# Linear attention feeding an MLP on one core: GpSimd waits for VectorE's two-input instructions, one more half block with seven products, and a new written order

## The chip, the cores and the metric

The kernel runs on one core of a Trainium2 chip. A core has five engines that run side by side, each through its own list of instructions in order: TensorE (PE in the profile) multiplies matrices into PSUM, VectorE (DVE) and ScalarE (ACT) work on PSUM and on SBUF, GpSimd (POOL) works on SBUF, and SyncE (SP) only starts DMAs here. They wait for one another by semaphores. The metric is device time in microseconds; lower is better. The median of three runs of the kernel before is 301.77 us (301.6 to 303.27).

## The reference

Eight batches of eight heads go through linear attention with positive random features, and the result through an MLP with x * relu6(x + 3) / 6. Shapes: q, k and v are 8 x 8 x 576 x 64, omega is 128 x 64, the MLP is 512 -> 2048 -> 512 over 8 x 576 = 4608 tokens.

```python
def phi(x):                                   # x is q or k, scaled by 64 ** -0.25
    h = einsum('bhsd,md->bhsm', x, omega) - sum(x * x) / 2
    return exp(h - max(h over m)) / sqrt(128)
kv = einsum('bhsm,bhsd->bhmd', phi(k), v)
z  = sum(phi(k) over s)
x  = einsum('bhsm,bhmd->bhsd', phi(q), kv) / (einsum('bhsm,bhm->bhs', phi(q), z) + 1e-6)
h  = x.reshape(4608, 512) @ w_in
out = (h * clip(h + 3, 0, 6) / 6) @ w_out
```

## The kernel before, in words

**Blocks.** Batch b gives 512 "main" tokens (block b of the MLP) and 64 left over; the left-over tokens of all batches form block 8. `attention(b)` writes the transposed attention output to `xT` (512 features in 4 tiles of 128, by 512 tokens) and the left-overs to `xS`. While TensorE works on the MLP of block b-1, the attention of batch b runs between.

**Attention.** `K`/`Q` (or the bursts `R`, from batch 3 on) project k and q onto omega, ScalarE takes the exponential (`kp`, `qpT`), VectorE the maximum (`mx`) and its reciprocal (`cc`). `vc` is v times `cc`, written by GpSimd or ScalarE, `kv` multiplies `kp` with it, `num` multiplies `qpT` with the result, and VectorE divides (`rec`, `div`). From batch 2 on, transposes are done by DMA, issued on SP.

**First MLP layer.** The 16 groups of 128 hidden units are `f` and `f + 8` for f = 0 to 7. Plainly (`mm1`, L1083) a group takes 4 matmuls of 128x512 and is followed by an activation on ScalarE into `tsb` (L1089) and a product on VectorE into `gT` (L1091). `mm1_quad` (L1248 for its matmuls) does two values of f and f + 8, on two halves of the tokens, by Strassen's method in Winograd's form: seven products of half size in the place of eight. It needs sums of weights (`input_sums`: W1 to W4, VectorE), sums of inputs (`x_sums`: X1 to X4), three copies (`q1`, `q2`, `q3`), two adds (`q4` L1273, `q5` L1276), and ends with four activations (`qr0` to `qr3`, L1284) and four products (`qg0` to `qg3`, L1286). It holds four PSUM banks of eight, X, Y, Z and W. `FIRST7 = (7, 2)` says from which block on: the half with f = 0 to 3 from block 7, the half with f = 4 to 7 from block 2.

**Second MLP layer.** Block 0 is done plainly (`mm2`, L1327). Later blocks use seven products too (`products`, L1415; the last one of block 8 at L1484): `token_sums` and `last_sum` make S1 to S4 out of `gT` (L1343, on GpSimd or VectorE), `plus` adds partial results (L1431), `store` writes out.

**Order.** Nothing is put in order on the chip. Each piece of work is an `Op` with its reads, its writes and an estimate of its time on each engine it may use. `ORDER` holds, for each engine, the numbers of the Ops in the order in which that engine does them; which list an Op is in also settles its engine. `schedule` walks through these lists with the estimates, gives out PSUM banks, and puts fill matmuls (L597) where it finds TensorE idle in the first 21 us. `emit` writes the instructions with a semaphore wait for each dependence that isn't already implied. An Op marked with `port` is one that the planner lets start only when a shared resource of VectorE and GpSimd is free:

```python
                if e in o.port:
                    shared[0] = o.end - (0.07 if e == "POOL" else 0.0)
```

That moves the planned start only; it leaves no wait in the program. DMAs of k and q for batches from 1 on are issued on GpSimd's queue, since they convert to bf16; loads of batches 3 to 7 wait for a named TensorE step of an earlier block (`gates`).

Of the kernel before, what the change touches and what calls it, by code (L numbers as in the profile page):

```python
# [16 lines left out]
EV0 = (("ACT","DVE"), ("ACT","DVE"), ("POOL", "ACT"), {"k": ("POOL", "ACT", "DVE"), "q": ("POOL", "ACT","DVE")})  # L17
# [4 lines left out]
        14, 121, 115, 117, 131, 138, 159, 147, 119, 141, 150, 144, 156, 135, 127, 153, 123, 125, 176, 129, 133, 174,  # L22
        166, 170, 172, 168, 188, 190, 203, 162, 178, 205, 164, 218, 193, 180, 220, 233, 208, 195, 235, 210, 407, 248,
        395, 223, 401, 198, 396, 238, 402, 397, 240, 408, 403, 398, 245, 225, 409, 404, 410, 213, 413, 416, 243, 228,
        271, 419, 291, 251, 422, 425, 428, 431, 275, 281, 434, 277, 437, 279, 318, 440, 443, 273, 309, 446, 315, 306,
        289, 285, 449, 312, 287, 297, 300, 586, 596, 303, 326, 320, 597, 336, 576, 294, 587, 330, 577, 588, 328, 283,
        578, 598, 332, 324, 589, 322, 599, 357, 579, 566, 359, 567, 362, 344, 580, 590, 568, 346, 334, 383, 569, 570,
        571, 349, 370, 385, 591, 365, 572, 581, 375, 372, 388, 600, 601, 592, 582, 583, 352, 391, 593, 573, 378, 602,
        603, 617, 505, 620, 614, 623, 466, 469, 475, 478, 635, 490, 472, 629, 632, 487, 481, 647, 484, 659, 644, 507,
        501, 653, 638, 497, 493, 668, 503, 499, 665, 662, 495, 650, 779, 511, 509, 531, 519, 780, 521, 536, 533, 524,  # L30
        789, 555, 782, 783, 560, 557, 790, 543, 712, 545, 548, 792, 793, 692, 795, 798, 799, 705, 796, 816, 810, 813,
        719, 819, 825, 828, 840, 831, 834, 845, 842, 844, 802, 863, 847, 803, 868, 849, 851, 865, 744, 870, 867, 732,
        987, 874, 737, 997, 734, 988, 872, 768, 756, 746, 1003, 749, 761, 990, 758, 998, 773, 770, 991, 1000, 1001, 900,
        1004, 1006, 1007, 913, 1018, 1024, 1021, 920, 1010, 1027, 1033, 927, 1039, 1050, 1048, 1036, 1011, 1042, 1053,
        1071, 1052, 1073, 1055, 1076, 1057, 1075, 952, 1059, 1078, 1080, 1195, 940, 976, 1082, 942, 957, 1196, 945, 954,
        1205, 964, 1198, 969, 966, 1199, 1206, 978, 981, 1121, 1208, 1209, 1108, 1214, 1215, 1128, 1229, 1232, 1226,
        1241, 1135, 1235, 1244, 1256, 1247, 1250, 1261, 1258, 1260, 1211, 1263, 1279, 1212, 1265, 1284, 1267, 1283,
        1281, 1218, 1286, 1403, 1404, 1290, 1148, 1160, 1219, 1150, 1165, 1288, 1184, 1162, 1153, 1406, 1413, 1414,
        1329, 1189, 1407, 1186, 1172, 1416, 1174, 1177, 1336, 1417, 1419, 1420, 1316, 1422, 1423, 1440, 1437, 1434,
        1452, 1464, 1449, 1443, 1466, 1468, 1469, 1458, 1455, 1471, 1426, 1473, 1427, 1343, 1475, 1487, 1356, 1611,  # L40
        1491, 1492, 1358, 1380, 1489, 1361, 1494, 1382, 1368, 1612, 1370, 1498, 1496, 1373, 1614, 1392, 1621, 1615,
        1622, 1537, 1394, 1397, 1385, 1624, 1625, 1544, 1627, 1628, 1551, 1630, 1634, 1631, 1524, 1635, 1642, 1645,
        1672, 1648, 1651, 1657, 1660, 1677, 1674, 1676, 1663, 1564, 1576, 1679, 1566, 1578, 1569, 1666, 1681, 1695,
        1581, 1683, 1588, 1699, 1600, 1590, 1697, 1593, 1700, 1722, 1702, 1602, 1723, 1605, 1704, 1706, 1753, 1732,
        1725, 1776, 1726, 1733, 1757, 1758, 1755, 1781, 1735, 1760, 1736, 1762, 1764, 1778, 1780, 1783, 1741, 1799,
        1742, 1787, 1785, 1738, 1804, 1801, 1824, 1803, 1806, 1822, 1739, 1808, 1810, 1826, 1827, 1745, 1876, 1829,
        1746, 1831, 1833, 1878, 1845, 1881, 1880, 1901, 1846, 1883, 1899, 1885, 1848, 1904, 1903, 1849, 1887, 1924,
        1906, 1922, 1908, 1855, 1927, 1926, 1856, 1910, 1929, 1945, 1858, 1931, 1949, 1933, 1950, 1859, 1861, 1947,
        1862, 1952, 1864, 1978, 1865, 1956, 1968, 1969, 1868, 1869, 1954, 1979, 1984, 1971, 1981, 1982, 1985, 1972,
        1988, 1989, 1997, 2003, 2000,  # L50
    ],
    "SP": [
        0, 18, 22, 33, 20, 23, 26, 25, 24, 27, 28, 32, 29, 30, 31, 262, 260, 261, 465, 464, 462, 463, 461, 459, 460,
# [72 lines left out]
        1390, 1462, 1485, 1619, 1463, 1509, 1640, 1638, 1641, 1560, 1575, 1559, 1574, 1562, 1654, 1402, 1587, 1586,  # L126
        1598, 1656, 1655, 1669, 1692, 1670, 1749, 1715, 1874, 1728, 1717, 1671, 1694, 1731, 1730, 1729, 1796, 1872,
        1797, 1873, 1819, 1875, 1774, 1844, 1821, 1843, 1896, 1898, 1851, 1897, 1775, 1919, 1853, 1852, 1921, 1854,
        1944, 1965, 1976,
    ],  # L130
}

# [288 lines left out]
def _emit(nc, es, q, k, v, omega, w_in, w_out, out):  # L421
# [803 lines left out]
    def mm1_quad(blk, f):  # L1225
# [11 lines left out]
        def bank(v):  # L1237
            return v.ring.t[v.slot]
# [373 lines left out]
```

## Time and profile before

| what | value |
|---|---|
| median of 3 runs | 301.77 us (301.6 to 303.27) |
| the profiled execution's own time | 302.46 us |
| its span, first to last instruction | 300.6 us |
| busy: PE / DVE / ACT / POOL | 292.2 / 271.4 / 212.9 / 206.3 us |
| matmuls | 2899 |
| granted TensorE clock | 1.00 |
| moved by DMA | 44.90 MB |

The span lies within the profiled execution's time. In the profile's groups, a name such as `p` or `gT` is a tile with its number left out, `p` being PSUM; `out<-in` says what is written from what. "Idle before" is the idle time of the engine just ahead of the instruction, with what ended it. A line number is that of the kernel before; one helper line can stand for several uses, so L1343 holds all sums of weights, inputs and hidden units, and L543/L544 all copies.

### The profile page before, as it was taken

What the parts mean: (1) busy time and instruction counts of PE and PEld (TensorE: products, weight loads), DVE (VectorE), ACT (ScalarE), POOL (GpSimd) and SP (SyncE); (2) the same over time, 40 slices, a digit from 0 to 9 for tenths busy, and PEclk for the clock granted to TensorE, in tenths of its full rate; (3) what the DMA queues carried; (4) which work ended last, traced back from release to release, by engine and by line L of the source; (5) the groups of instructions that cost most, each with busy time, mean ns of one, the idle gap of its engine ahead of it and who ended that gap; (6) DMA issues with size and microseconds to landing.
All of it is one profiled execution on the core that took longest, in us unless ns stands there. A gap on an engine that the chain in (4) does not pass through costs nothing.

```text
span 300.6 us, 7551 instructions
## 1 busy us (share of the span) xinstructions
PE 292.2 (97%) x2899; PEld 222.1 (74%) x2899; DVE 271.4 (90%) x593; ACT 212.9 (71%) x479; POOL 206.3 (69%) x226
## 2 busy tenths in 40 slices
PE   7999999999999999999989999999999999999996
PEld 5688955554884798569736887588757788888885
DVE  4889898889999998999879998999999999997875
ACT  2975899199878992997587776985887576687310
POOL 1664827039898986589939869998279939869711
PEclk9999999999999999999999999999999999999999
DMA  7999999999999997799769898999531600300034
GB/s 234 292 188 168 266 200 127 197 215 155 242 110 234 126 191 138 173 139 196 171 169 172 144 241 129 106 200 220 86 94 57 166 0 3 126 16 0 2 143 140
DMA packets 90100, 44.90 MB, mean 149 GB/s; under 512 B 57936, under 2 KB 87760, under 8 KB 90064
## 3 DMA queue, kind: packets, MB, share of 16 engines
q1 hardware_dynamic: 62064, 30.71, 46.1%
q0 software_dynamic: 26592, 12.46, 33.7%
q10 hardware_dynamic: 1408, 1.25, 1.3%
q8 instruction: 23, 0.38, 0.5%
q14 instruction: 13, 0.11, 0.1%
HBM read 36.73 MB, written 9.44 MB: 154 GB/s over the span
## 4 chain that ended last, share of the span: by engine, by line
PE 81%; DVE 8%; ACT 5%; POOL 5%; issue 1%; POOLq 0%
PE p L1415 29%; PE p L1248 15%; PE p L1083 11%; PE p L1327 5%; PE p L1302 4%; PE p L1014 3%; PE p L986 2%; DVE mx L820 2%; PE p L796 2%; POOL s L1343 2%; PE p L597 2%; ACT kp L847 2%; PE p L860 2%; POOL vc L970 1%; PE p L840 1%; PE p L799 1%
## 5 line engine op out<-in xcount | busy, mean ns | idle before, releaser
L1284 ACT ACTIVATE tsb<-p 128x512 f16<-128x512 f32 x72 | 41.4, 601 | 21.8 <-PE p L1248 12.0
L1083 PE MATMUL p<-xT,wi 128*128 128x512 f16 x224 | 53.1, 379 | 1.8 <-ACT qpT L824 1.4
L1286 DVE SCALAR_TENSOR_TENSOR gT<-tsb,p 128x512 f16<-128x512 f16 x72 | 46.8, 676 | 3.0 <-ACT tsb L1284 2.8
L1415 PE MATMUL p<-wo,gT 128*128 128x256 f16 x368 | 47.0, 273 | 0.0
L1083 PEld LDWEIGHTS p<-xT,wi 128*128 128x128 f16 x224 | 21.3, 98 | 24.9 <-ACT qpT L824 2.1
L1091 DVE SCALAR_TENSOR_TENSOR gT<-tsb,p 128x512 f16<-128x512 f16 x56 | 36.4, 674 | 3.1 <-ACT tsb L1089 2.8
L1415 PEld LDWEIGHTS p<-wo,gT 128*128 128x128 f16 x368 | 34.8, 98 | 4.9 <-issue 0.5
L1089 ACT ACTIVATE tsb<-p 128x512 f16<-128x512 f32 x56 | 33.2, 620 | 7.0 <-PE p L1083 5.3
L543 ACT COPY p<-p 128x512 f32<-128x512 f32 x55 | 32.2, 599 | 4.1 <-PE p L1415 2.0
L970 POOL TENSOR_TENSOR vc<-v,cc 128x512 bf16<-128x512 f32 x27 | 28.7, 1061 | 7.1 <-DVE cc L964 5.2
L824 ACT ACTIVATE qpT<-p 128x512 bf16<-128x512 f32 (+1 forms) x50 | 27.7, 577 | 6.8 <-PE p L799 6.8
L1343 POOL TENSOR_TENSOR gT<-gT,s 128x512 f16<-128x512 f16 x21 | 24.3, 1157 | 12.0 <-PE p L1415 10.6
L1415 PE MATMUL p<-t,gT 128*128 128x256 f16 x256 | 31.8, 273 | 0.4 <-DVE u L1431 0.4
L1343 POOL TENSOR_TENSOR gT<-gT 128x512 f16<-128x512 f16 x24 | 28.2, 1177 | 4.7 <-DVE s L1343 3.2
L815 ACT ACTIVATE kp<-p 128x512 bf16<-128x512 f32 (+1 forms) x50 | 26.8, 571 | 5.9 <-PE p L799 5.6
L820 DVE TENSOR_REDUCE mx<-kp 128x4 f32<-128x512 bf16 (+1 forms) x50 | 29.3, 618 | 0.3 <-ACT kp L815 0.3
L643 POOL DMA_DIRECT2D kb<-in_k_dram x21 | 16.2, 774 | 18.8 <-PE p L1083 18.1
L1030 DVE TENSOR_TENSOR xb<-p,rec 128x384 f16<-128x384 f32 (+1 forms) x64 | 28.2, 467 | 0.3
L1415 PEld LDWEIGHTS p<-t,gT 128*128 128x128 f16 x256 | 24.3, 98 | 5.4 <-issue 1.3
L1343 POOL TENSOR_TENSOR s<-gT,s 128x512 f16<-128x512 f16 x21 | 24.4, 1164 | 3.4 <-DVE s L1343 2.2
L1343 POOL TENSOR_TENSOR s<-gT 128x512 f16<-128x512 f16 x19 | 22.0, 1158 | 4.7 <-DVE gT L1286 3.1
L643 POOL DMA_DIRECT2D qb<-in_q_dram x28 | 19.6, 713 | 7.5 <-PE p L1083 5.0
(139 smaller groups left out, 671.4 us busy)
## 6 DMA issues: line engine op xcount, KB each, us to landing
v<-in_v_dram SPq DMA_DIRECT2D x14, 512.0 KB, 4.8
out_dram<-osb SPq DMA_DIRECT2D x14, 512.0 KB, 3.3
kb<-in_k_dram POOLq DMA_DIRECT2D x14, 256.0 KB, 5.0
qb<-in_q_dram POOLq DMA_DIRECT2D x14, 256.0 KB, 5.6
wo<-in_moe_w_out_dram POOLq DMA_DIRECT2D x8, 256.0 KB, 9.9
wi<-in_moe_w_in_dram POOLq DMA_DIRECT2D x3, 512.0 KB, 7.5
q<-in_q_dram SPq DMA_DIRECT2D x4, 256.0 KB, 4.8
vl<-in_v_dram SPq DMA_DIRECT2D x8, 128.0 KB, 4.2
```

The source lines that it names most:

```text
L543: return E.copy(dst(), src())
L643: lambda E: E.dma_start(dst, src), prio + 0.001 * turn_of[0], reads=gate, writes=keys,
L820: op("DVE", dvet(128 * (d1 - d0)), lambda E, ko=ko, mo=mo: E.reduce_max(mo, ko, axis=AX.X), p0 + 0.01, reads=[("kp", 0, d, lh) for d in ra ...
L970: return E.tensor_tensor(vcm[:, :, 0:D], v32[:, m, :, :], cbc, ALU.mult)
L1083: ins = E.matmul(ring.t[vh.slot], wi[:, c, 128 * f:128 * f + 128], xv[:, c, :], start=(c == 0), stop=(c == NJ - 1))
L1089: op("ACT", actt(512), lambda E: E.activation(tsb[tu][:], ring.t[vh.slot], AF.Relu, bias=0.5, scale=1.0 / 6.0), t - 0.1, reads=[vh], write ...
L1091: op("DVE", dvet(512), lambda E: E.scalar_tensor_tensor(gT[gu][:, f, :], tsb[tu][:], 1.0, ring.t[vh.slot], ALU.min, ALU.mult), t - 0.1, re ...
L1248: ins = E.matmul(bank(v)[:, 256 * g:256 * g + 256], w(c, f + g), x[:, c, :], start=start and g == 0 and c == 0, stop=c == 1, skip_group_ch ...
L1284: op("ACT", actt(512), lambda E, v=v, tu=tu: E.activation(tsb[tu][:], bank(v), AF.Relu, bias=0.5, scale=1.0 / 6.0), t - 0.1, reads=[v], wr ...
L1286: op("DVE", dvet(512), lambda E, v=v, tu=tu, dst=dst: E.scalar_tensor_tensor(dst, pieces(tsb[tu][:]), 1.0, pieces(bank(v)), ALU.min, ALU.m ...
L1343: op(engines, {"POOL": 0.1 + n / 475.0, "DVE": 0.09 + n / 2000.0}, lambda E: E.tensor_tensor(dst, x, y, ALU.subtract if minus else ALU.add ...
L1415: ins = E.matmul(ring.t[v.slot][:, 256 * j:256 * j + 256], a[:, f, 128 * j:128 * j + 128], w[:, f, :], start=(first and f == 0 and j == 0) ...
```

## The change

1. `schedule` remembers the last VectorE Op that is marked with `port` (`holder`). A GpSimd Op with `port` that the walk puts after it, and within 4 us of its end, gets a dependence on it, which `emit` turns into a semaphore wait where no other wait covers it. GpSimd is also planned to start 0.15 us after such a VectorE Op.
2. `FIRST7` and `QUAD` go from (7, 2) to (7, 1): the half with f = 4 to 7 of block 1 is done by `mm1_quad`. The sums of its weights are made before.
3. `q5` writes its sum to the SBUF tile `p7` and no longer to PSUM bank W; `qr2` and `qg2` read it there, and `qg2` is marked with `port="DVE"`.
4. In batch 0, `vc` is made in two halves, each on GpSimd, VectorE or ScalarE.
5. The loads of batches 3 to 7 lose their `gates`.
6. Several estimates of time change, and `ORDER` is a new one for all five engines.

```diff
-EV0 = (("ACT","DVE"), ("ACT","DVE"), ("POOL", "ACT"), {...})
+EV0 = (("ACT","DVE"), ("ACT","DVE"), ("POOL", "ACT", "DVE"), {...})
 ORDER = {
...
+        holder = None
...
                 if e in o.port:
-                    shared[0] = o.end - (0.07 if e == "POOL" else 0.0)
+                    shared[0] = o.end - (0.08 if e == "POOL" else -0.15)
+                    if e == "DVE":
+                        holder = o
+                    elif holder is not None and st - holder.end < 4.0:
+                        o.deps.setdefault(holder, False)
...
-        op(EV_VC if b else V0, {...}, e_vc, t, port=("POOL", "DVE"), reads=[("cc", pb, m), ("v32", 0, m), ("v32", 1, m)], writes=[("vc", u2, 0)], name="vc" + nm)
+        for hs in ([0], [1]) if b == 0 else ([0, 1],):
+            i0, i1 = 4 * hs[0], 4 * hs[-1] + 4
...
-    FIRST7 = (7, 2)
-    QUAD = (7, 2)
+    FIRST7 = (7, 1)
+    QUAD = (7, 1)
...
-            return v.ring.t[v.slot]
+            return v.ring.t[v.slot] if isinstance(v, Virt) else p7[v[1]][:]
...
-        op("DVE", dvet(512), lambda E: E.tensor_tensor(bank(W), bank(Z), p7[w7][:], ALU.add), t - 0.1, reads=[("p7", w7), Z], writes=[W],
-           name="q5." + nm)
+        op("DVE", dvet(512), lambda E: E.tensor_tensor(p7[w7][:], bank(Z), p7[w7][:], ALU.add), t - 0.1, reads=[Z],
+           writes=[("p7", w7)], name="q5." + nm)
...
-        for n, (v, i, k_) in enumerate(((X, 0, 0), (Y, 1, 0), (W, 1, 1), (Z, 0, 1))):
+        for n, (v, i, k_) in enumerate(((X, 0, 0), (Y, 1, 0), (("p7", w7), 1, 1), (Z, 0, 1))):
...
-               t - 0.1, reads=[v, ("t", tu)], writes=[...], name="qg%d.%s" % (n, nm))
+               t - 0.1, reads=[v, ("t", tu)], writes=[...], name="qg%d.%s" % (n, nm),
+               port="DVE" if n == 2 else ())
...
-            load(b, (), {"k": [("m1", b - 2, 2)], "q": [("m1", b - 2, 4)], "v": [("m1", b - 2, 9)]})
+            load(b, (), {t: [] for t in "kqv"})
...
+            for h in range(2):
+                if FIRST7[h] == 1:
+                    input_sums(h)
```

## The prediction

> **What bounds the kernel now.** I read the page first: busy shares, then the 40 slices, then the idle time by stretch, then the waits of TensorE alone.
>
> ```profile
> span 300.6 us, 7551 instructions
> PE 292.2 (97%) x2899; PEld 222.1 (74%) x2899; DVE 271.4 (90%) x593; ACT 212.9 (71%) x479; POOL 206.3 (69%) x226
> PE   7999999999999999999989999999999999999996
> DVE  4889898889999998999879998999999999997875
> ```
>
> TensorE (PE) is full from the second slice to the last but one, VectorE (DVE) is at 90%, and ScalarE (ACT) and GpSimd (POOL) have room. A busy TensorE need not run at its pace, so I compare instruction starts: a 128x512 matmul follows the one before after 0.216 us, a 128x256 one after 0.109 us. In the chain of work that ended last, eight 128x256 matmuls take 0.87 us, or 0.109 us each. TensorE's stream sets the time, and what can be won is a shorter stream or fewer holes in it. The holes, by stretch of the span (columns: length, then busy us of each engine):
>
> ```profile
> 0.00:22.50 22.50, 20.16 (x204) 15.60 (x205) 15.95 (x51) 14.85 (x35) 11.64 (x21) 1.00 1.07 238
> 60.00:150.00 90.00, 89.83 (x907) 64.77 (x906) 85.23 (x188) 74.13 (x174) 71.85 (x76) 1.00 1.04 174
> 150.00:240.00 90.00, 87.48 (x908) 64.39 (x906) 84.88 (x188) 68.39 (x153) 68.20 (x74) 1.00 0.81 149
> 292.50:300.60 8.10, 5.30 (x57) 4.59 (x54) 4.71 (x9) 0.00 (x0) 1.16 (x1) 1.00 0.40 130
> 60.00:94.00 34.00, 34.00 (x307) 22.29 (x306) 31.71 (x68) 29.97 (x70) 25.86 (x28) 1.00 1.05 191
> ```
>
> Of 8.4 us without a matmul, 2.3 lie in the start, 2.8 in the tail, and about 3.2 inside, most of them in 150 to 240 us. What ended them, in TensorE's waits:
>
> ```profile
> PE p L1083 <- ACT qpT L824: 1.4, 1, 1.4
> PE p L1415 <- POOL s L1343: 0.7, 1, 0.7
> PE p L1083 <- DVE gT L1091: 0.4, 1, 0.4
> PE p L1415 <- DVE u L1431: 0.4, 1, 0.4
> ```
>
> A hole hides some 0.16 us more, since the matmul ahead of it is drawn 0.27 us long at a pace of 0.11. Six holes are then worth 3.2 + 1.0 = 4.2 us. They come from VectorE, GpSimd or ScalarE being late. One cause of lateness can be seen directly:
>
> ```profile
> 237.97 1.16 POOL L1343 TENSOR_TENSOR q<-xT 128x512 f16<-128x512 f16 x1
> 238.19 1.22 DVE L1343 TENSOR_TENSOR s<-gT,s 128x512 f16<-128x512 f16 x1
> ```
>
> VectorE's sum takes 0.41 us where GpSimd is quiet. Here GpSimd started 0.22 us earlier, and the sum ends 0.28 us after GpSimd does. The same happens at 278.94 us (1.41 us), just ahead of the hole that `u` ends. The 55 two-input sums of 512 elements on VectorE (L1343) cost 30.8 us, not 55 x 0.41 = 22.7: 8.1 us are lost in this way, 0.15 us per sum.
>
> **The change part by part.**
>
> *Seven products in the second half of block 1's hidden units.* TensorE loses 32 matmuls of 128x512 and gains 56 of 128x256 by the two programs' instruction lists: 32 x 0.216 = 6.91 against 56 x 0.109 = 6.10, so 0.81 us less on the path. No clearing matmul is added. The weight sums W1 to W4 were there before; W1 of this half (at 88 us, 0.68 us of VectorE) only moves ahead. New on other engines: four adds `q4`, `q5` (4 x 0.69), four input sums (X2, X3 on VectorE, X1, X4 on GpSimd at 1.16 each) and six copies on ScalarE (0.60 each, 3.6 us, while 3 output copies of block 0 leave that stretch). From the first to the second block's first `gT` write VectorE has 72 instructions, not 65. At the pace of 0.60 us of back-to-back instructions the extra is 4 x 0.60 for the adds, 1.7 for two S1 sums, one S4 and one X2, 0.6 for X1 of the next block, 0.6 for one more maximum, less W1 and two `kvz`: about 4.0 us. VectorE idles 34.00 - 31.71 = 2.3 us in 60 to 94 us. So it becomes full there, and a lateness of up to 1.7 us, 2.5 us with the shorter TensorE stretch, has to be made good later. This is the dear part.
>
> *`q5` writes p7 in SBUF instead of the PSUM bank W; `qr2`, `qg2` read it there (20 each).* The bank comes free after `q3`, not after `qg2`, a gain that I can't price alone. ScalarE's 20 activations read SBUF. The near rows are 128x64 from SBUF at 342 ns and 128x130 from PSUM at 276; less 0.79 ns an element (`qpT`: 618 ns for 512, 416 for 256), the fixed parts are 291 and 173 ns, so 0.12 us more each. The Trainium skill ("VectorE: DVE Perf Modes", The TRN2 errata) gives ScalarE 224 cycles of fixed cost from SBUF and 172 from PSUM, 0.04 us more each. By the row that is 2.4 us, by the page 0.9 us, both over 300 us of an engine with 88 us idle; I take the row, since it holds this kernel's form with a scale, and charge the path nothing. On VectorE the page would make `qg2` 62 cycles cheaper from SBUF, 20 x 0.065 = 1.3 us. The rows deny it: 128x256 from PSUM (409 ns) and an unhindered 128x512 two-input sum from SBUF at two elements a cycle (410) have the same fixed part. I take 0.
>
> *Waits.* GpSimd instructions that wait on VectorE go from 54 to 83 of some 147 computing ones. A GpSimd start follows the VectorE end that it waits for by 0.07 us (a sum at 283.87 of 0.41 us, GpSimd at 284.35), so 29 x 0.07 = 2 us of GpSimd, beside its 94 idle ones; its instructions fall by some 10 us besides (12 fewer 512-element sums of gT and s at 1.16). Behind a waiting instruction stand the next sums and the k and q loads on the same queue; those loads now have no TensorE gate (18.1 + 5.0 us of waits before), so they come no later. If that cover is gone, a late S sum holds TensorE as at 238 us. What the waits buy: GpSimd no longer takes the port ahead of a VectorE instruction that stands before it. The Trainium skill ("SBUF — State Buffer", Who interferes with whom) says that a VectorE instruction with two SBUF inputs contends with GpSimd's reads, and that the first to issue holds the pair. The row at 238 us agrees, and the page speaks against one part: `qg2` now has two SBUF inputs, where before one lay in PSUM. At 0.15 us each that is 20 x 0.15 = 3.0 us new blocking against 8.1 us of old, of which waits can remove only what GpSimd took out of turn. Taking a half, 4 us, the two nearly cancel: -1 us of VectorE in sum, from +3 (nothing removed) to -8 (all removed, `qg2` free).
>
> *New sequence.* VectorE's instruction counts by their rows give about +3 us (4 fewer PSUM copies in the products, 10 fewer copies of transposes, 4 new adds, 12 more S sums), ScalarE +10 us, GpSimd -10 us. The start keeps its TensorE work and gets 3 more fill matmuls (3 x 0.11 = 0.3 us of idle that they cover), while two ScalarE copies of 1.05 us (`vcl`) leave the chain at 12.9 us for GpSimd. Bounds of its effect are -1.0 and +1.0 us; I take 0. The tail can be read: before, the last TensorE instruction ended at 297.80 us, its VectorE part at 298.13, the last store was issued by 298.71. Afterwards the second half of product 5 stands only one 0.45 us product ahead of the end, so C21 (0.69 us) ends 0.44 us after TensorE, and its two stores (0.57 us each, both on SP) are out 0.47 + 1.14 = 1.6 us after it instead of 0.9: +0.7 us on the path (bounds 0.2 and 0.9). SP keeps its 114 instructions; loads, transposes and stores swap places by one or two. No wait of TensorE on a transpose of x or of k and q is in the list above, so that is hidden; if one came late, it would cost up to the 1.2 us that such a transpose takes to issue on SP.
>
> *Holes.* The 4.2 us inside are partly port blocking (238, 280 and, behind GpSimd's DMA issues, 160 us: 1.5 us + 3 x 0.16 = 2.0) and partly the burst of projections at 152 us (1.4 us), which has to find banks. Freed banks and ordered ports speak for fewer, the fuller VectorE for more. I take 1.9 us recovered, between 4.2 and -4.
>
> Sum against the profiled execution: 300.6 - 0.8 + 0.7 + 0 - 1.9 = 298.6 us span. The profiled execution took 302.46 us, 1.9 over its span, and the median of the three runs is 301.77. I put the same -2.0 on the median: **299.8 us**.
>
> **The rivals.**
> 1. *The gain is spent.* The products give 0.8, the tail takes 0.7 back, and holes move instead of closing, 4 us as before: 301.8 - 0.8 + 0.7 = 301.7 us (300.3 to 303.2). For it: the burst at 152 us is tied to ScalarE, which gets 10 us more. Against it: two of the holes are plainly port blocking.
> 2. *VectorE becomes the bound in block 1 (slower).* Place: from the first `gT` of block 1 to its products, 60 to 94 us. Excess 2.5 us as above, plus 7 new two-input instructions x 0.15 = 1.0, gives 3.5; TensorE pays what the following stretches can't absorb, and VectorE is as full there (85.23 of 90 us). It decides when more than about 1.6 us stay unpaid beyond what other holes give back. At 3.0 us unpaid and nothing won elsewhere: 301.8 - 0.8 + 0.7 + 3.0 = 304.7; with 1 us won elsewhere 303.7 us.
> 3. *All holes close.* 301.8 - 0.8 + 0.7 - 3.8 = 297.9 us. Against it: GpSimd's DMA issues get no wait.
> 4. *The waits do nothing*, because GpSimd seldom stood ahead of its turn: then 3.0 us of new `qg2` blocking is left, and the result is that of rival 1 or 2.
>
> **How the numbers follow.** Forecast 0.48 (298.6 to 301, five sixths of it faster), rival 1 0.20, rival 2 0.26, rival 3 0.06; rival 4 is inside 1 and 2. A measurement of this kernel tells about 0.5%, or 1.5 us: faster is below 300.26, slower above 303.28. Faster: 0.40 + 0.06 + 0.02 = 0.48; within: 0.08 + 0.16 + 0.01 = 0.25; slower: 0.02 + 0.25 = 0.27. The range for 8 in 10 is 298.0 to 304.2, since cases of both signs are large; the forecast's own is 298.6 to 301.
>
> **What would show it.** Right: TensorE busy near 290.5 us with holes of about 2 us between 22 and 292 us; S sums on VectorE near 0.45 us in the mean instead of 0.56; GpSimd waits released by VectorE's L1343 sums and `qg2`; `qr2` near 0.7 us; 1.6 us from TensorE's end to the last store's issue. Wrong: a wait of TensorE on `gT` or an S sum between 65 and 100 us, `qg2` above 0.8 us in the mean, GpSimd idle ahead of S sums with TensorE waiting for them, or a first MLP matmul later than 21 us.

## The result, and the profile after

The changed kernel takes 300.25 us (299.76 to 300.67), the kernel before in the same comparison 302.03 us (301.6 to 303.27). The ratio is 0.9935, with a 95% interval of 0.9913 to 0.9957: 0.65% faster. The profiled execution took 300.11 us, its span is 298.3 us; before it was 302.46 and 300.6 us.

The head of the page of the kernel after, with busy shares and TensorE's 40 slices:

```profile
span 298.3 us, 7663 instructions
PE 291.8 (98%) x2926; PEld 225.9 (76%) x2926; DVE 270.0 (91%) x597; ACT 219.7 (74%) x499; POOL 193.9 (65%) x217
PE   7999999999999999999989999999999999999995
```

TensorE is as full as it was. GpSimd lost 12.4 us of work, ScalarE gained 6.8, and VectorE stayed near where it was (271.4 before). Idle time by stretch (columns: length, then busy us of TensorE, its weight loads, VectorE, ScalarE and GpSimd, the granted clock, the DMA share and GB/s):

```profile
0.00:22.50 22.50, 20.69 (x199) 15.49 (x200) 15.16 (x49) 15.53 (x39) 11.12 (x22) 1.00 1.08 241
60.00:94.00 34.00, 33.92 (x336) 24.74 (x335) 32.11 (x73) 28.36 (x65) 25.35 (x30) 1.00 1.12 184
60.00:150.00 90.00, 89.90 (x935) 67.08 (x934) 84.93 (x194) 74.59 (x174) 68.26 (x77) 1.00 1.08 185
150.00:240.00 90.00, 88.99 (x928) 67.30 (x926) 84.63 (x190) 72.12 (x168) 65.97 (x67) 1.00 0.71 141
290.00:298.30 8.30, 4.76 (x52) 4.20 (x49) 4.18 (x8) 0.00 (x0) 0.49 (x1) 1.00 0.39 126
```

The gap of 2.5 us in 150 to 240 us has shrunk to 1.0. In 60 to 94 us, where seven products are new, TensorE has no hole worth the name and VectorE still idles 1.9 us. The waits of TensorE alone (us in total, times, longest):

```profile
PE p L603 <- DVE fill L598: 1.5, 1, 1.5
PE p L802 <- ACT qpT L830: 0.8, 1, 0.8
PE p L728 <- DMA q<-in_q_dram: 0.2, 1, 0.2
PE p L1429 <- DVE s L1357: 0.2, 1, 0.2
```

The first belongs to the start and stood there before. Of the holes inside, one of 0.8 us at 151 us is left; those that ended at 238 us (GpSimd's sum), at 281 us (`u`) and at 152.9 us (1.4 us) are gone. A part of the cause is in VectorE's groups of sums (L1357 was L1343), and in its products (L1299 was L1286):

```profile
L1299 DVE SCALAR_TENSOR_TENSOR gT<-tsb,p 128x512 f16<-128x512 f16 x80 | 54.1, 696 | 0.9 <-ACT tsb L1297 0.5
L1357 DVE TENSOR_TENSOR gT<-gT 128x512 f16<-128x512 f16 x13 | 7.0, 542 | 0.0
L1357 DVE TENSOR_TENSOR gT<-gT,s 128x512 f16<-128x512 f16 x13 | 6.5, 501 | 0.0
L1357 DVE TENSOR_TENSOR s<-gT,s 128x512 f16<-128x512 f16 x15 | 6.0, 411 | 0.0
L1357 DVE TENSOR_TENSOR s<-gT 128x512 f16<-128x512 f16 x14 | 5.7, 410 | 0.0
```

Most sums now take 0.41 us. Over all 66 sums of 512 elements on VectorE, the time beyond 0.417 us each adds up to 2.65 us; for the 55 of the kernel before it was 7.9 us. The sums took 0.457 us in the mean, where they had taken 0.56. Something is lost still: GpSimd starts a sum by itself, since it waited for TensorE and not for VectorE, and VectorE's next sum runs into it. In the timeline of the kernel after, of VectorE and then of GpSimd (start, length, instruction):

```profile
286.14 1.37 DVE L1357 TENSOR_TENSOR gT<-gT,s 128x512 f16<-128x512 f16 x1
288.04 1.22 DVE L1357 TENSOR_TENSOR gT<-gT 128x512 f16<-128x512 f16 x1
...
286.09 1.15 POOL L1357 TENSOR_TENSOR gT<-gT,s 128x512 f16<-128x512 f16 x1 [9.45 <-PE p L1429]
287.83 1.15 POOL L1357 TENSOR_TENSOR gT<-gT,s 128x512 f16<-128x512 f16 x1 [0.60 <-PE p L1429]
```

The change puts a wait in only where the plan has VectorE first, so it leaves such cases alone.

The books of the two profiled executions: TensorE's last matmul ends at 294.76 us, not 297.80, so 3.04 us earlier; what follows it takes 3.55 us, not 2.81, so 0.74 more; the span is 2.3 us shorter.

### The profile page after: what moved, and what is told of

Its sections match the earlier page's. It is cut to its first block, busy times and chain, and to the rows that moved or that the text cites. A ratio compares the mean times of both kernels' runs of the same rounds, so it can differ in the third digit from the quotient of the medians.

```text
span 298.3 us, 7663 instructions
## 1 busy us (share of the span) xinstructions
PE 291.8 (98%) x2926; PEld 225.9 (76%) x2926; DVE 270.0 (91%) x597; ACT 219.7 (74%) x499; POOL 193.9 (65%) x217
## 3 DMA queue, kind: packets, MB, share of 16 engines
q10 hardware_dynamic: 1408, 1.18, 1.3%
## 4 chain that ended last, share of the span: by engine, by line
PE 88%; ACT 7%; DVE 3%; issue 0%; DVEq 0%
PE p L1429 30%; PE p L1261 20%; PE p L1096 12%; PE p L1316 5%; PE p L1341 5%; PE p L1027 3%; PE p L999 3%; PE p L802 2%; ACT kp L853 2%; PE p L603 2%; PE p L805 2%; ACT tsb L1102 1%; ACT qpT L870 1%; PE p L866 1%; PE p L846 1%; DVE gT L1299 1%
## 5 line engine op out<-in xcount | busy, mean ns | idle before, releaser
L1297 ACT ACTIVATE tsb<-p 128x512 f16<-128x512 f32 x80 | 48.1, 630 | 12.1 <-PE p L1261 6.0
L1299 DVE SCALAR_TENSOR_TENSOR gT<-tsb,p 128x512 f16<-128x512 f16 x80 | 54.1, 696 | 0.9 <-ACT tsb L1297 0.5
L1096 PE MATMUL p<-xT,wi 128*128 128x512 f16 x192 | 46.1, 379 | 0.0
L549 ACT COPY p<-p 128x512 f32<-128x512 f32 x65 | 39.4, 623 | 7.6 <-PE p L1261 6.1
L1357 POOL TENSOR_TENSOR gT<-gT,s 128x512 f16<-128x512 f16 x19 | 21.9, 1155 | 19.7 <-PE p L1429 11.7
L1104 DVE SCALAR_TENSOR_TENSOR gT<-tsb,p 128x512 f16<-128x512 f16 x48 | 31.4, 675 | 1.5 <-ACT tsb L1102 1.2
L1096 PEld LDWEIGHTS p<-xT,wi 128*128 128x128 f16 x192 | 17.9, 98 | 18.4 <-issue 0.8
L1102 ACT ACTIVATE tsb<-p 128x512 f16<-128x512 f32 x48 | 28.6, 648 | 3.9 <-PE p L1096 3.6
L981 POOL TENSOR_TENSOR vc<-v,cc 128x512 bf16<-128x512 f32 (+1 forms) x27 | 26.6, 984 | 7.2 <-PE p L1001 1.5
L830 ACT ACTIVATE qpT<-p 128x512 bf16<-128x512 f32 (+1 forms) x50 | 27.4, 593 | 2.0 <-PE p L805 1.8
L1357 POOL TENSOR_TENSOR s<-gT,s 128x512 f16<-128x512 f16 x17 | 19.6, 1155 | 9.4 <-DVE gT L1299 4.4
L1357 POOL TENSOR_TENSOR gT<-gT 128x512 f16<-128x512 f16 x19 | 22.0, 1156 | 4.3 <-DVE s L1357 2.0
L1357 POOL TENSOR_TENSOR s<-gT 128x512 f16<-128x512 f16 x18 | 20.8, 1155 | 5.8 <-DVE gT L1299 3.2
L870 ACT ACTIVATE qpT<-p 128x512 bf16<-128x512 f32 (+1 forms) x30 | 16.9, 608 | 2.8 <-PE p L866 2.5
```

The lines of the kernel that those rows point to most:

```text
L549: return E.copy(dst(), src())
L830: op("ACT", actt(128 * (d1 - d0)), lambda E, lh=lh, part=part: E.activation(qd[:, part[0]:part[1], lh, :], out_of(part, 1, lh)[0].rearrang ...
L1096: ins = E.matmul(ring.t[vh.slot], wi[:, c, 128 * f:128 * f + 128], xv[:, c, :], start=(c == 0), stop=(c == NJ - 1))
L1102: op("ACT", actt(512), lambda E: E.activation(tsb[tu][:], ring.t[vh.slot], AF.Relu, bias=0.5, scale=1.0 / 6.0), t - 0.1, reads=[vh], write ...
L1104: op("DVE", dvet(512), lambda E: E.scalar_tensor_tensor(gT[gu][:, f, :], tsb[tu][:], 1.0, ring.t[vh.slot], ALU.min, ALU.mult), t - 0.1, re ...
L1297: op("ACT", actt(512), lambda E, v=v, tu=tu: E.activation(tsb[tu][:], bank(v), AF.Relu, bias=0.5, scale=1.0 / 6.0), t - 0.1, reads=[v], wr ...
```

## The experiments

Ratios are to the kernel before, measured in the same comparison; its own median was 302.39, 302.29, 301.96 and 301.46 us in the four comparisons, so times of different comparisons can't be set side by side to a few tenths. For most of these runs I matched each matmul with the same matmul in the trace of the kernel it was made from, and took the difference of their starts. The difference stays constant wherever nothing happens and steps where something does, so it shows what an edit cost and where. (Two executions of the same program differ by a constant from the start on: see the last section.) In us, at some places in the span of the trace that stands under "against":

```
at us                                25     60     70     80     90    110    150    170    200    260    285
against the kernel after:
  a_again    (unaltered)            0.22   0.23   0.23   0.24   0.23   0.24   0.24   0.24   0.24   0.24   0.24
  a_nowait   (no waits)            -0.01   0.00   0.01   0.01   1.51   6.03   6.95   7.29   9.54  10.46  10.46
  a_noqgwait (none for qg2)         0.48   0.48   0.48   0.48   0.48   0.48   0.48   0.49   0.47   1.04   1.04
  a_pe8      (+1.73 us TensorE)    -0.38  -0.38   0.87   1.00   0.99   0.99   0.99   1.00   0.99   1.00   1.00
  a_dve4     (+2.7 us VectorE)      0.34   0.34   0.34   2.24   2.24   2.24   2.24   2.24   2.25   2.25   2.25
  a_dve4_g   (+2.7, at qg)         -0.38  -0.37  -0.37   0.93   1.60   1.60   1.60   1.60   1.59   1.60   1.60
  a_pe8_b3   (+1.73 in block 3)     0.09   0.09   0.09   0.09   0.09   0.09   1.82   1.82   1.81   1.82   1.82
  a_dve4_b3  (+2.7 in block 3)     -0.34  -0.34  -0.34  -0.34  -0.34  -0.34   1.79   1.79   1.78   1.78   1.78
against the kernel before:
  before_again (unaltered)          0.40   0.66   0.66   0.66   0.66   0.67   0.68   0.18   0.18   0.20   0.20
  b_wait     (the waits alone)      0.59   0.59   0.59   0.59   0.59   0.37   0.53  -1.91  -1.50  -1.36  -1.95
against before_again:
  b_wait_again (the waits alone)   -0.46  -0.72  -0.72  -0.72  -0.72  -0.94  -0.65  -1.42  -1.21  -1.12  -1.72
```

**The kernel after once more.** It is the base for the others, unaltered.

> The changed kernel unaltered, as the yardstick for the other runs on the same chip. All theories: ratio to the kernel before 0.991 to 0.996, span near 298.3 us.

It took 300.16 us (299.82 to 300.49), ratio 0.9931 [0.9904, 0.9957], with a span of 298.5 us. The sums of VectorE lost 2.8 us in that trace, and the tail was 3.54 us: the reading of the trace above repeats.

**The waits alone, in the old order.** The kernel before gets the dependences on the VectorE instruction ahead, and nothing else:

```diff
+        holder = None
...
+                    if e == "DVE":
+                        holder = o
+                    elif holder is not None and st - holder.end < 4.0:
+                        o.deps.setdefault(holder, False)
```

> The kernel before with the dependence of GpSimd on the last VectorE port instruction as the one change; its order and estimates stay. Theory (the waits close holes of whatever sequence): the 8.1 us lost by VectorE's L1343 sums fall to 5 us or less and the time falls by 0.5 to 1.5 us. Rival (the old order was made for GpSimd without these waits, which delay it): time unchanged or up to 1 us longer, the lost time still falls.

It took 300.56 us (299.68 to 301.6), ratio 0.9947 [0.9928, 0.9965], at first sight nearly the whole gain. Planned starts and banks are those of the kernel before; by the two programs' lists, 30 instructions of GpSimd wait for something else than they did, and one of ScalarE's waits falls away as implied. TensorE ends at 295.85 us with a tail of 2.80; VectorE's sums lost 4.95 us, 2.9 less than before. The shift has these steps: -0.2 us at 95, -1.43 at 152.9, -0.57 at 160.6, -0.43 at 166, then 0.4 back, and -0.59 at 281. The steps at 160 and 281 have a cause in VectorE's sums: those of 1335 ns at 158.3 us and of 1411 ns at 278.9 us in the kernel before are not blocked here. The largest step has none there. The waits of TensorE in this run:

```profile
PE p L602 <- DVE fill L597: 1.5, 1, 1.5
PE p L1420 <- POOL s L1348: 0.7, 1, 0.7
PE p L865 <- ACT qpT L869: 0.7, 1, 0.7
```

The hole that ends with GpSimd's sum (0.7 us, at 238 us in the kernel before) is still there, so not every hole was VectorE's blocking: waits don't close this one, only the new order does. The hole at 152.9 us is absent. My prediction had read it as the burst of projections, held by ScalarE. By the program, the matmul that stood there (L1083, the first of block 4) waits for an activation that was over by about 151.0 us, and for the four transposes of x. The last two transposes of x of block 4 in the kernel before (length of the issues on SP, their starts; then the times from issue to landing, the longer of which belongs to the later one):

```profile
L1059 SPq DMA_TRANSPOSE xT<-xb x2: 1254/1332/1410, 146.8 to 148.2; - x2
DMA to landing us min/median/max: 2.5/3.6/4.6
```

148.2 + 4.6 = 152.8 us: the hole ends with the last transpose. In the run with the waits the same two landed after 2.5 and 2.6 us. Is that the waits' doing, or chance? Both kernels were run once more, unaltered.

**Both once more.**

> The kernel before, unaltered, for a second trace. In its first trace TensorE stood still for 1.4 us until 152.9 us; the profile names an activation as its cause, but by the program's own waits the matmul that stood needs an earlier activation (over by about 151.0 us) and the last transpose of x, which was issued at 148.2 us and landed 4.6 us later, at 152.8. If that late landing belongs to the kernel before, it is here again: 4 us or more, and a hole above 1 us. If it was the chance of one execution, it lands after 2.5 to 3 us as the other transposes there do, there is no such hole, and the span is about 1.4 us shorter than 300.6, apart from the start.

> The kernel before with the waits alone, unaltered, for a second trace. In its first the same transpose landed after 2.6 us and there was no hole at 152 us; of the 2.5 us that TensorE gained, 1.4 lay there. If the waits do it, it is so again and the two kernels differ by 1.8 us as before. If it is chance, the landing can be long here too, and what the waits surely give is the rest, 1.1 us (0.6 at 160 us, 0.4 at 166, 0.6 at 281, less what is lost between).

The kernel before took 301.35 us (300.53 to 303.4), ratio 0.9998 [0.9982, 1.0014]; the one with the waits 300.44 us (299.61 to 301.46), ratio 0.9968 [0.9954, 0.9982]. The same two transposes in the second trace of the kernel before:

```profile
L1059 SPq DMA_TRANSPOSE xT<-xb x2: 1260/1288/1317, 147.6 to 148.9; - x2
DMA to landing us min/median/max: 2.6/3.3/4.1
```

and in the second trace with the waits:

```profile
L1064 SPq DMA_TRANSPOSE xT<-xb x2: 1260/1294/1327, 147.0 to 148.4; - x2
DMA to landing us min/median/max: 2.6/3.4/4.2
```

The hole is back in both, 0.9 and 1.1 us, and the profile puts it down to another activation than the first time:

```profile
PE p L1083 <- ACT kp L815: 0.9, 1, 0.9
```

```profile
PE p L1088 <- ACT kp L820: 1.1, 1, 1.1
```

In the three traces that have the hole, the matmul behind it starts 0.09 us after that landing (152.84 and 152.93, 153.02 and 153.11, 152.62 and 152.71 us); in the fourth the transpose landed at 151.15 us and there is no hole. So the hole is the transpose's, and it comes back with the waits in place: it isn't the waits that closed it. Over all 14 traces here this last transpose of block 4 landed 4.1 to 4.6 us after its issue, but for the 2.5 us of that fourth trace, the first with the waits, which was the lucky one. Taking the hole out makes the traces agree. From its first MLP matmul to its end TensorE needs 277.66 and 277.46 us in the two traces of the kernel before; less 1.43 and 0.93 us for that hole (by the steps of the shift), and 0.27 in the second for an activation late once at 28 us, that is 276.2 and 276.3. With the waits it needs 275.11 and 276.20; less 0 and 1.18, that is 275.1 and 275.0. **The waits alone are worth 1.2 us**, for 2.7 to 2.9 us that VectorE no longer loses. The two ratios, 0.53% and 0.32% of 302 us, make it 1.6 and 1.0. The kernel after needs 273.84 and 273.86 us. Its order issues the last transpose 0.7 us earlier (at 147.5 us), and although that one lands after 4.4 us too, no hole is left at its end in the traces of that order.

**The rest of the change, without the waits.** The kernel after loses the last two lines of the diff above; products, tiles, loads and order stay.

```diff
-                    elif holder is not None and st - holder.end < 4.0:
-                        o.deps.setdefault(holder, False)
```

> The changed kernel without the dependence of GpSimd on the last VectorE instruction that shares the port; all else, the order of every engine included, stays. Theory (the waits keep GpSimd from taking the port out of turn, and that closes holes of TensorE): time lost by VectorE's L1357 sums beyond 0.42 us each rises from 2.9 us to 5 us or more, TensorE's idle time between 60 and 290 us from 1.1 to 2 us or more, and the time by 0.8 to 2 us. Rival (the new sequence alone did it, the waits are idle): time within 0.4 us of the changed kernel, sums as before.

It took 311.75 us (309.51 to 313.07), ratio 1.0308 [1.0266, 1.0349]: 11.6 us slower than with the waits, where I had expected 0.8 to 2, and 9.4 us slower than the kernel before. The head of its page, and the largest waits of TensorE inside:

```profile
span 308.8 us, 7648 instructions
PE 295.3 (96%) x2921; PEld 225.4 (73%) x2926; DVE 279.9 (91%) x597; ACT 220.5 (71%) x499; POOL 198.7 (64%) x217
```

```profile
PE p L1427 <- DVE s L1355: 2.9, 3, 1.9
PE p L1094 <- DVE mx L824: 2.8, 1, 2.8
```

VectorE's busy time rose by 9.9 us for the same instructions. Its sums lost 13.5 us, 19 of 66 taking over 480 ns; `qg2` lost 2.8. One such pair in the timeline, VectorE and then GpSimd:

```profile
87.09 1.33 DVE L1355 TENSOR_TENSOR gT<-gT 128x512 f16<-128x512 f16 x1
...
86.97 1.16 POOL L1355 TENSOR_TENSOR gT<-gT,s 128x512 f16<-128x512 f16 x1
```

GpSimd was 0.12 us ahead, and VectorE's sum took 0.92 us too long. Blocked sums hold TensorE at once: one from 83.17 us took 1.73 us and ended at 84.90 us; the matmul that needs it starts at 84.95 us after a wait of 0.8 us. Two of 1.21 and 1.27 us in a row end at 184.77 us, and a matmul starts at 184.82 us after a wait of 1.9 us.

The other large wait, 2.8 us, is not what the profile calls it. By the program the matmul that stands there, the first of its block, needs the four transposes of x, and the last of them was issued at 89.85 us and landed after 7.0 us, at 96.89 us, where the kernel after has 4.0:

```profile
96.98 2.68 PE L1094 MATMUL p<-xT,wi 128*128 128x512 f16 x8 [2.83 <-DVE mx L824]
L1070 SPq DMA_TRANSPOSE xT<-xb x1: 1194/1194/1194, 89.8 to 89.8; - x1
DMA to landing us min/median/max: 7.0/7.0/7.0
```

The matmul starts 0.09 us after the landing, as in the three holes above. The issue came 1.9 us later than in the kernel after because VectorE was late: it followed a division that ended at 89.82 us. Why the landing took 3 us longer is open, with one trace. Behind this hole the granted clock fell to one half from 97.9 to 101.3 us, the only time after the start, in any of the traces, that this happened during TensorE's work (columns as in the first table of idle time):

```profile
94.00:97.00 3.00, 0.17 (x3) 0.05 (x2) 2.71 (x5) 2.07 (x4) 0.03 (x1) 1.00 1.38 142
98.00:101.00 3.00, 3.00 (x13) 1.47 (x10) 0.67 (x2) 1.20 (x2) 2.84 (x4) 0.50 1.07 391
```

There 128x512 matmuls follow one another after 0.43 us, not 0.22, and TensorE falls another 1.6 us behind. So of the 6.0 us that the table has at 110 us, 1.5 were there at 90 us, 2.9 are the hole and 1.6 the clock.

Over the whole span VectorE lost 12.2 us more than with the waits (10.9 in sums, 1.3 in `qg2`), and TensorE came 10.46 us later, 4.5 us of it by that one landing and the clock behind it. That the new order needs the waits doesn't hang on these: of the six runs the fastest, at a mean clock of 0.999, still took 309.51 us.

So the parts don't add. The waits alone: 1.8 us faster in this comparison, 1.2 by the traces once the landing of the transpose is taken out. The rest alone: 9.4 slower. Both: 2.2 faster (medians 302.39 before, 300.56, 311.75, 300.16). Why the old order loses so much less without waits (7.9 us of VectorE, not 13.5) I can only argue: the new one puts instructions where they fit if GpSimd waits.

**No waits for `qg2`.** In the kernel after, GpSimd waits for VectorE's sums and its copies to `xT`, but not for `qg2`; by the program's list four waits of 83 go.

```diff
-                    if e == "DVE":
+                    if e == "DVE" and not o.name.startswith("qg"):
```

> The kernel after, but GpSimd doesn't wait for qg2 (only for VectorE's sums and its copies to xT): the qg2 are still in SBUF on both sides. My prediction put the new blocking of qg2 at 0.15 us each, 3.0 us in all; with the waits it came to 1.5 us (mean 753 ns beside 676 of the other gT products). Theory (the waits also guard qg2, and what one loses is passed on): qg2's loss goes up towards 3 us or more, and the time rises by 0.3 to 1.5 us over the kernel after, to 300.5 to 301.7. Rival (the sums' waits do it all; four of 83 waits are too few): no change, 300.0 to 300.4, with qg2 as before.

It took 300.73 us (300.25 to 301.18), ratio 0.9956 [0.9939, 0.9973]. The lost time of `qg2` went from 1.5 to 2.8 us, just as without any waits: two more of the twenty were blocked, one of them here (VectorE's row holds two products, the first of them `qg2` with 1342 ns):

```profile
250.33 1.94 DVE L1299 SCALAR_TENSOR_TENSOR gT<-tsb,p 128x512 f16<-128x512 f16 x2
...
249.97 1.15 POOL L1357 TENSOR_TENSOR gT<-gT,s 128x512 f16<-128x512 f16 x1
251.20 1.48 POOL L1357 TENSOR_TENSOR s<-gT 128x512 f16<-128x512 f16 x1
```

The shift steps at 235 and 250 to 255 us, where these two lie, by 0.56 us in all: 1.2 us of VectorE cost 0.56 us of TensorE. The theory holds, near its lower end. The rival is out by the trace, in which `qg2` does lose more; the times alone don't settle it, since the two intervals overlap.

**More TensorE work in block 1.** To see whether TensorE or VectorE sets the pace where seven products are new, each of block 1's two quads gets two fill matmuls ahead of `qa` and two ahead of `qw`.

```diff
+                if start and blk == 1:
+                    for _ in range(2):
+                        E.matmul(bank(v), fill[:, 0:128], fill[:], start=True, stop=True)
```

> The kernel after, with two fill matmuls of 128x512 added ahead of qa and ahead of qw in each of the two quads of block 1: eight matmuls of 0.216 us, 1.73 us more of TensorE's own work, nothing left out. Theory (TensorE sets the end in block 1, VectorE keeps up): the time rises by the whole work, 1.5 to 1.9 us over the kernel after of 300.2, so 301.7 to 302.1, with TensorE's end that much later. Rival (VectorE is the bound in block 1, TensorE has cover there): at most 0.5 us, 300.2 to 300.7.

It took 301.58 us (301.09 to 302.46, but for two of 22 runs at 306), ratio 0.9979 [0.9967, 0.9991]. By the shift, the 1.73 us cost 1.38. Most of the rest, 0.24 us, went into a wait of the kernel after ahead of a projection at 71 us. The result is just below the theory's band and far above the rival's.

**More VectorE work in block 1.** One maximum over a 128x512 tile ahead of each `q4` and `q5` of block 1.

```diff
+        def more(E):
+            if blk == 1:
+                i = unused.pop()
+                E.reduce_max(spent[:, i:i + 1], fill[:], axis=AX.X)
+            return E
...
-           lambda E: E.tensor_tensor(bank(Y), bank(Y), p7[w7][:], ALU.add)
+           lambda E: more(E).tensor_tensor(bank(Y), bank(Y), p7[w7][:], ALU.add)
... (the same for q5)
```

> The kernel after, with one maximum over a 128x512 tile in SBUF (about 0.6 us, one SBUF operand, its result read by nobody) ahead of each of the four adds q4 and q5 of block 1: about 2.4 us more of VectorE's work in 60 to 94 us, nothing left out. VectorE has 34.0 - 32.1 = 1.9 us idle there and 5 us in 60 to 150. Theory (VectorE has slack behind its buffers): the time rises by less than 0.8 us, 300.2 to 301.0. Rival (VectorE is the bound in block 1): it rises by 1.5 to 2.4 us, 301.7 to 302.6, with TensorE waiting on gT or on S sums of VectorE.

It took 301.99 us (301.63 to 302.37), ratio 0.9990 [0.9975, 1.0004]. The group of the maxima, and the new wait of TensorE:

```profile
L1255 DVE TENSOR_REDUCE spent<-fill 128x1 f32<-128x512 bf16 x4 | 2.7, 667 | 0.0
```

```profile
PE p L1269 <- DVE p L1297: 0.6, 1, 0.6
```

My theory fails here. 2.7 us of VectorE made TensorE 1.90 us later, all of it between 72 and 80 us. Only 0.8 us was absorbed, though VectorE idles 1.9 us in the stretch. So both engines are at their limit in block 1: TensorE has 0.35 us to spare, VectorE 0.8.

**The same, out of the way of `q4` and `q5`.** Is it the latency of those two adds, or VectorE as a whole? The maxima move ahead of `qg1` and `qg3`.

```diff
-            op("DVE", dvet(512), lambda E, v=v, tu=tu, dst=dst: E.scalar_tensor_tensor(
+            op("DVE", dvet(512), lambda E, v=v, tu=tu, dst=dst, n=n: (more(E) if n % 2 else E).scalar_tensor_tensor(
```

> The same four extra maxima in block 1, one SBUF operand each, 0.667 us and so 2.7 us in sum, but ahead of qg1 and qg3 instead of q4 and q5: still in the same two quads, now outside the chain from TensorE over q4 and q5 back to TensorE. Nothing is left out. Ahead of q4 and q5 they moved TensorE's later matmuls by 1.9 us, all of it between 65 and 82 us. If VectorE as a whole is full in block 1 (VectorE sets the pace over some 10 us), the shift is again 1.5 to 2.2 us. If only the step from q4 and q5 to the next matmuls is tight, it is below 0.7 us.

It took 302.11 us (301.7 to 302.57), ratio 1.0010 [0.9991, 1.0029]. The shift is 1.97 us, again of 2.7. The waits of TensorE have moved with the maxima:

```profile
PE p L1437 <- DVE gT L1307: 0.9, 2, 0.5
```

It is VectorE as a whole, wherever the work is put in.

**The same in block 3.** Both additions, each in a run of its own, in a block that had these quads in the kernel before. Against the runs in block 1 one number changes; for the matmuls:

```diff
-                if start and blk == 1:
+                if start and blk == 3:
```

> The eight extra matmuls of 128x512 (1.73 us) in block 3's two quads instead of block 1's, where they moved what follows by 1.38 us; nothing is left out. If TensorE alone sets the pace in block 3, the shift is 1.5 to 1.8 us; if VectorE is level with it there too, 1.0 to 1.5 us.

> The four extra maxima ahead of q4 and q5 in block 3 instead of block 1; nothing is left out. Block 3 had these quads in the kernel before too. If only block 1, where the new quads stand, has VectorE at its limit, the shift of TensorE's matmuls after block 3 is below 0.7 us. If every quad with attention around it is as tight (VectorE at 84.6 of 90 us in 150 to 240), it is 1.5 to 2.2 us as in block 1.

The matmuls: 301.68 us (301.45 to 302.18), ratio 0.9999 [0.9982, 1.0015], a shift of 1.73 us, all that was put in. The maxima: 302.24 us (301.86 to 303.78), ratio 1.0010 [0.9996, 1.0024], a shift of 2.13 us of 2.7. So block 1 is nothing special: in block 3, too, TensorE sets the pace, and VectorE has some 0.6 us of room.

**A shorter tail.** The kernel after, with its last few steps in another order: TensorE does both halves of product 5 ahead of the three pieces that come last, VectorE makes C21 as soon as it can, and two of the last stores change places between SyncE's and ScalarE's queues.

```diff
 "PE":  -  2006, 2009, 2024, 2012, 2021, 2013, 2027
        +  2006, 2009, 2012, 2013, 2024, 2021, 2027
 "DVE": -  2010, 2011, 2025, 2022, 2014, 2028
        +  2010, 2011, 2014, 2025, 2022, 2028
 "SP":  -  2023, 2017, 2018          "ACT": -  2016, 2026, 2029
        +  2017, 2018, 2029                 +  2016, 2026, 2023
```

> The changed kernel with another order of the last seven TensorE pieces and of what follows them: both halves of product 5 ahead of the three pieces of the last product, C21 right after them on VectorE, its stores first on SP. Theory (the tail costs 0.7 us because C21 ends late and its two stores follow on one queue): span from TensorE's end falls from 3.5 to 2.9 us and the time by 0.4 to 0.7 us. Rival (the tail is set by the last store alone, which is no earlier): time unchanged within 0.2 us.

It took 299.51 us (299.43 to 300.26), ratio 0.9915 [0.9890, 0.9940]. The ends of the two chains of work, of the kernel after and then of this one (start, length, what):

```profile
293.44 0.89 PE p L1429 x8
294.32 0.02 issue
294.35 0.69 DVE osb L1445
```

```profile
292.96 1.22 PE p L1497 x14
...
294.21 0.42 DVE osb L1505
294.63 0.02 issue
294.66 0.29 DVE osb L1505
```

C21 of 0.69 us is no longer last; a piece of 0.29 us is. From TensorE's end to the end of the span it takes 3.12 us, not 3.55 (2.9 was expected); TensorE itself, counted from its first MLP matmul, ends 0.1 us later, so the trace gains 0.33 us. Its median is the lowest of all, 0.65 us below the kernel after in the same comparison, as expected; against the kernel before the gain is plain, against the kernel after the intervals of the two ratios overlap.

Not tried: the new order with `q5` in a PSUM bank, the old one with `q5` in `p7`, and the new one with the loads gated. Each order depends on which banks and tiles are free when, so each of these would need an order of its own. What `q5`, the loads and the halves of `vc` are worth apart from the order therefore stays open.

## Why the prediction was right, and where it wasn't

The forecast of 299.8 us is 0.45 below the measured 300.25, inside its own range of 298.6 to 301; its direction is right. The sum of steps came to 298.6 us of span, and 298.3 was measured. That closeness is in part luck: the holes gave some 1 us more than I had taken, the start took 0.8 us more, and the two nearly cancel. Step by step it is less good than the sum.

- *What bounds it: TensorE's stream, VectorE with some idle time.* Half right. Extra TensorE work costs 80 to 100% of itself, but extra VectorE work costs 70 to 79%. In the quads the two are level to within a microsecond, in block 1 and block 3 alike. "DVE 90%" should have been read as a second bound.
- *The holes' causes.* The largest, 1.4 us at 152 us, I put down to the burst and to ScalarE, and said of the transposes of x that none holds TensorE, since none is in the list of waits. This step failed: it was one of them, landing 4.6 us after its issue, under the name of an activation. The waits that the program states, and the times to landing, would have told. The hole at 238 us, which I called port blocking, failed too: with the waits alone it stays, at 0.7 us, while those at 160 and 281 us, 0.4 each, go.
- *Holes: 1.9 of 4.2 us recovered.* From its first MLP matmul to its end TensorE gained 3.8 us on the first trace of the kernel before, 3.6 on the second. Less 0.81 for the products that is 3.0 or 2.8 us. The waits account for 1.2 of it; the rest belongs to the new order and what goes with it, the hole at the late transpose included. What that is above my figure, 0.9 to 1.1 us, made good a start that I had at nothing.
- *Seven products, -0.81 us.* Only the counts show it, 56 short matmuls for 32 long ones. The rate found in block 1 (1.38 us of time for 1.73 of matmuls) would make it 0.65 us; it was not measured by itself. TensorE was busy for 291.8 us, not near 290.5 as I had said.
- *VectorE full in block 1: +4.0 us against 2.3 idle.* The mechanism was right, the size wrong, and this was called the dear part. By the start of each instruction, 60 to 94 us held 36.1 us of VectorE's work before and 37.5 after: +1.4. The four adds came as I had them (2.73 us), the input sums at 0.83. But six S sums had cost 4.05 us there, and nine now cost 3.67: unblocked, they more than paid for three new ones. W1 and W2 moved ahead (-1.36), a product, a maximum and two `kvz` fewer took off another 1.87, and a weight sum and an output copy added 1.36. I charged the new sums to this stretch and credited the unblocking to another step. By the 0.8 us of room that the added maxima found, a true +4 us would have brought rival 2; that is an inference, no run shows it.
- *`qr2` from SBUF, +0.12 us each.* Wrong, and the page was right. `qr2` took 652 ns in the mean and 635 in the median, where the other three took 622 and 602: 0.03 us more, beside an estimate of 0.04 from the cycles that the Trainium skill ("VectorE: DVE Perf Modes", The TRN2 errata) gives. The rows I chose compared different shapes. Nothing hung on it.
- *`qg2` no cheaper from SBUF.* Right: 684 ns in the median, the others 678. The page's 62 cycles less don't show in this kernel.
- *Waits: 8.1 us of blocking halved, 3.0 new on `qg2`, -1 us in sum.* The direction was right. The old blocking (55 x 0.41 is 22.55, so my 8.1 should have been 8.3; beyond 0.417 us each it is 7.9) fell by two thirds, to 2.65 us, and `qg2` lost 1.5 us, not 3.0: three of twenty were blocked, at 899, 968 and 1670 ns. That is -3.7 us of VectorE. The Trainium skill's rule ("SBUF — State Buffer", Who interferes with whom: the first to issue holds the shared pair) is what the rows show at 87, 250 and 286 us; how often, only a run tells. Without the waits on `qg2` its blocking is 2.8 us, near the 3.0 said.
- *New sequence: start 0, tail +0.7.* The tail was read well: 0.74 us more, and 1.5 us from TensorE's end to the last store's issue where 1.6 was said. The start cost 0.45 us: the first MLP matmul came at 20.92 us instead of 20.15, of which 0.34 is the longer first transposes of k, a matter of when TensorE's pace doubles in that execution (last section) and not of the order. Less the length of these transposes it comes at 18.2 us in all four traces of the old order, and at 18.65 in the two of the kernel after.
- *Waits and sequence costed apart.* The sequence was given bounds of -1 and +1 us. Without the waits it costs 9.4 us in the medians; in the one trace some 4.5 us of that hang on a transpose's landing and the clock behind it. The step took for granted that the new order stands on its own; it doesn't.

Of the rivals, the first (gain spent, holes only moved) is out: TensorE's idle time inside fell from 3.2 to 1.1 us. The third is out by the start and by the hole left at 151 us. The fourth (waits do nothing) is refuted by the waits alone and by the order without them. The second did not come about (33.92 of 34 us busy in block 1), but 0.8 us of room is all that stood between the change and it.

## What to carry to other kernels

A written order that counts on who goes first at a shared port must enforce it with a wait, and order and waits are to be costed together. A few microseconds of extra work on one engine, put in one place, with the shift of matched instructions against the unaltered trace, tell how much room that engine has; busy shares don't. Where a hole is put down to an engine that had been done for long, compare with the landing of the DMAs that the same instruction waits for, and take a second trace before pricing it. A long hole can cost more than its length: look at the granted clock just behind it.

## What the runs showed of the hardware

- *The start is not the same twice, and it is the clock.* TensorE's first 14 transposes of k begin at 4.98 us in every trace and take 1.88 to 2.88 us, with hardly a wait between them. The fill matmuls of 128x256 ahead of them follow one another after 0.213 us, those later in the span after 0.109. In the ten traces in which the transposes have this step, from 0.21 to 0.11 us, it comes between 5.2 and 7.4 us; in nine of them the profile's record of a full clock begins within 0.07 us of it (5.79 and 5.85 us in the kernel after, 7.35 and 7.37 without the waits for `qg2`), the tenth has no record. In the other four the record begins before 4.98 us and the transposes take 1.9 us. Every later matmul moves with this: by 0.24 us between the two executions of the kernel after, by 0.40 us between those of the kernel before, and from -0.38 to +0.48 us among kernels with the same start.
- *The clock can fall again behind a hole.* Without the waits it was 0.50 for 3.4 us, from 1 us after a hole of 2.8 us on, and cost 1.6 us. No hole of 1.9 us or less in these traces was followed by that.
- *A transpose by DMA lands after 2.4 to 7.0 us*, counted from the start of its issue, over the 24 of x in each of 14 traces. The last one of x in block 4 took 4.6 and 4.1 us in the kernel before, 2.5 and 4.2 with the waits alone, in the same order.
- *A blocked VectorE instruction waits out nearly all of the other's.* A sum on VectorE that starts while GpSimd still has over 0.2 us of a computing instruction ahead of it ends 0.28 us after that instruction does (0.275 to 0.290 us in 113 of 114 such cases in the 14 traces; in the one other it wasn't blocked). The longest `qg2`, 1670 ns beside 684, began 0.03 us after a GpSimd sum of 1155 ns (at 171.52 and 171.49 us). It took 1655 to 1670 ns in every trace of this order where it was looked up, with waits and without. While GpSimd only issued a DMA, 15 of 15 sums of the kernel after took 0.39 to 0.42 us; without the waits 6 of 14 took 0.8 to 1.7 us, and why is open.
- *Blocked time isn't time.* A microsecond of VectorE's blocking was worth 0.4 us (the waits alone: 1.2 for 2.8), 0.45 (`qg2` unguarded: 0.56 for 1.24) and 0.5 us (no waits: 10.46 for 12.2, less the 4.5 us of the one landing and the clock), according to where it fell.
